# Projecting queries and keys head by head in float32 matmuls of 64 rows

## The chip, the cores and the metric

One core of a Trainium2 chip runs the whole program. The metric is the device time of one execution in microseconds (us); the kernel before takes 731.62 us (median of three runs, 731.14 to 731.96).

## What is computed

Linear attention with a feature map, then two feed-forward stages, on the attention's output laid out as 1152 tokens by 512. All of it is float32, and the last stage's shapes do not matter for this change.

```python
def phi(x):
    proj = np.einsum('bhsd,df->bhsf', x, w_phi)          # head_dim 64 -> 128 features
    proj = proj - np.max(np.abs(proj), axis=-1, keepdims=True)
    return np.concatenate([np.exp(proj), np.exp(-proj)], axis=-1)
q_p, k_p = phi(q), phi(k)                                 # batch 2, heads 8, seq 576
kv = np.einsum('bhsf,bhsd->bhfd', k_p, v)
z = np.sum(k_p, axis=2)
num = np.einsum('bhsf,bhfd->bhsd', q_p, kv)
den = np.einsum('bhsf,bhf->bhs', q_p, z)[..., None] + 1e-06
attn = num / den                                          # -> x, 1152 x 512
y = (x @ w_a * (x @ w_b)) @ w_out                         # d_ff 1536
out = sum over e of p[:, e:e+1] * (max(y @ w1[e], 0) @ w2[e])   # 4 experts
```

## The kernel before

Heads are handled two at a time: a pair p of heads lies one head in partitions 0 to 63, the other in 64 to 127, so that a tile of 128 tokens of one pair is a 128 x 128 block with the head dimension on the partitions. The keys and the queries come in `load_chunk` as chunks of 768 columns; an *item* is 256 columns of a chunk, that is two such tiles j. There are 36 items, 18 of keys (`kind` "k") and then 18 of queries. 576 tokens are four tiles of 128 and a rest of 64, and the rests of two pairs share one tile (marked "m" in `tiles_of_batch`).

The main loop at the end goes over *slots*, and in every slot writes, in this order: the splitting of the raw columns of the item three slots ahead (`split_x`), the projection of this slot's item (`stage_proj`), the key-value sums of the item three slots back (`stage_kv`), for queries the transposes of the item four slots back (`stage_rt`), then what was put off to this slot (`stage_kvz`, `stage_num`, `stage_x`, `stage_xparts`), and in even slots three tasks that prepare later weights (`prep(3)`: ACT, DVE and POOL work on a 512-column half). Every engine takes its instructions in the order in which this loop writes them.

`split_x` makes from each item's float32 columns a high part (ACT, line 84) and a low part (POOL, line 85) in the fast float32r type. `stage_proj` then makes one product of 128 rows against a block-diagonal weight of 256 columns (`wbp`: w_phi for head 0, zeros, and the reverse) out of three float32r matmuls, hi x hi, hi x lo, lo x hi, so that both heads come out of one matmul (lines 166 to 168):

```python
nc.tensor.matmul(out=o, lhsT=hi, rhs=wbp[:, 0], start=True, stop=False)
nc.tensor.matmul(out=o, lhsT=hi, rhs=wbp[:, 1], start=False, stop=False)
nc.tensor.matmul(out=o, lhsT=lo, rhs=wbp[:, 0], start=False, stop=True)
```

DVE takes the largest magnitude (line 171) and subtracts it (line 173); for keys ACT makes two exponentials (lines 179 and 180). `stage_kv` (line 197) sums into PSUM with true float32 matmuls; a full tile uses 128 rows, a shared rest first rows 0 to 63 for both heads of one pair, then rows 64 to 127 for both heads of the next. A float32 matmul is two instructions on PE, a float32r matmul or a transpose is one. When a pair is done, DVE copies its sums out of PSUM (`kvt`, line 207), two slots later PE transposes them (line 218) and DVE (batch 0) or ACT (batch 1) copies them again (`kvz`, lines 221 and 223). Four PSUM buffers ("u") serve the projections, the transposes and the first matmuls of the next stage by turns; two more ("nd") hold the sums. After the loop the two feed-forward stages run as long series of float32r matmuls.

Of the kernel before, what the change touches and what calls it, by code (L numbers as in the profile page):

```python
# [9 lines left out]
F32 = mybir.dt.float32  # L10
F32R = mybir.dt.float32r
U32 = mybir.dt.uint32
AF = mybir.ActivationFunctionType
ALU = mybir.AluOpType
# [33 lines left out]
def tile_linear_attention_then_mlps(ctx, tc, qT, kT, v, w_phi, wab, wout, w12, probs, out):  # L48
# [19 lines left out]
    m_p = None  # L68
    l_p = None

    wb = r_p.tile([128, 2, 128], F32, tag="wb", name="wb")
    wbp = r_p.tile([128, 2, 256], F32R, tag="wbp", name="wbp")

    with tc.manual_schedule():
        nc.scalar.dma_start(out=wb[0:64, 0, :], in_=w_phi)
        nc.scalar.dma_start(out=wb[64:128, 1, :], in_=w_phi)
        nc.vector.memset(wb[0:64, 1, :], 0.0)
        nc.vector.memset(wb[64:128, 0, :], 0.0)

        nc.vector.memset(psm, 0.0)  # L80
        nc.scalar.activation(out=psm, in_=psm, func=AF.Exp)
# [1 line left out]
        def two_parts(hi, lo, src, eng):  # L83
            nc.scalar.activation(out=hi, in_=src, func=AF.Copy)  # L84
            eng.tensor_tensor(out=lo, in0=src, in1=hi.bitcast(F32), op=ALU.subtract)  # L85

        NC = 3 * 256
        xraw = {}
        xpart = {}

        def load_chunk(n):


            if n >= 2 * B * 3:
                return
            t = r_p.tile([128, NC], F32, tag="xraw", name="xraw", bufs=2)
            src = (kT if n < B * 3 else qT)[n % (B * 3)]
            step = 256 if n == 0 else NC
            for c in range(0, NC, step):
                nc.sync.dma_start(out=t[:, c:c + step], in_=src[:, c:c + step])  # L100
            xraw[n] = t

        def split_x(i, eng):
            n, c = i // 3, i % 3 * 256
            if c == 0:
                xpart[n] = [r_p.tile([128, NC], F32R, tag=f"xp{k}", name="xp", bufs=2) for k in range(2)]
            hi, lo = (t[:, c:c + 256] for t in xpart[n])
            if i == 0:
                nc.vector.tensor_copy(hi, xraw[n][:, 0:256])
                nc.vector.tensor_tensor(out=lo, in0=xraw[n][:, 0:256], in1=hi.bitcast(F32), op=ALU.subtract)  # L110
            else:
                two_parts(hi, lo, xraw[n][:, c:c + 256], eng)
            if c == 512:
                load_chunk(n + 2)

        vt = {}

        def alloc_v(b):
            t = k_p.tile([128, 5, NP, 192], F32, tag="v", name="v", bufs=2)
            nc.gpsimd.memset(t[:, :, :, 64:128], 1.0)  # L120
            vt[b] = t

        def load_v(b, st):

            rows = v[b, st * 128:min(S, (st + 1) * 128)]
            n = rows.shape[0]
            for lo in range(0, 128, n):
                o = vt[b][lo:lo + n, st].rearrange("p a c -> p (a c)")
                nc.sync.dma_start(
                    out=o[:, 128:128 + 3 * 192].rearrange("p (a c) -> p a c", c=192)[:, :, 0:128],  # L130
                    in_=rows[:, 1:H - 1, :].rearrange("s (a h) d -> s a (h d)", h=2),
                )
                nc.sync.dma_start(
                    out=o.rearrange("p (a c) -> p a c", c=64)[:, 0:4 * NP - NP:3 * NP - 1, :],
                    in_=rows[:, 0:H:H - 1, :],
                )
# [10 lines left out]
        for kind in "kq":  # L147
            for b in range(B):
                for g in range(9):
                    items.append((kind, b, g, seq[2 * g:2 * g + 2]))  # L150

        st_r = {}
        st_kp = {}
        kv_ps = {}
        kvt_t = {}
        kvz_t = {}
        qp_t = {}

        def stage_proj(i):
            kind, b, g, ts_ = items[i]  # L160
            ps = u_p.tile([128, 2, 2, 128], F32, tag="u", name="pj")
            for j in range(2):
                c = i % 3 * 256 + j * 128
                hi, lo = (t[:, c:c + 128] for t in xpart[i // 3])
                o = ps[:, j].rearrange("p h f -> p (h f)")
                nc.tensor.matmul(out=o, lhsT=hi, rhs=wbp[:, 0], start=True, stop=False)
                nc.tensor.matmul(out=o, lhsT=hi, rhs=wbp[:, 1], start=False, stop=False)
                nc.tensor.matmul(out=o, lhsT=lo, rhs=wbp[:, 0], start=False, stop=True)
            ps4 = ps.rearrange("p t h f -> p (t h) f")
            mx = r_p.tile([128, 4], F32, tag="mx", name="mx", bufs=4)  # L170
            nc.vector.tensor_reduce(out=mx, in_=ps4, op=ALU.max, axis=AX.X, apply_absolute_value=True)
            r = r_p.tile([128, 4, 128], F32, tag="r", name="r", bufs=6)
            nc.vector.tensor_tensor(
                out=r, in0=ps4, in1=mx.unsqueeze(2).to_broadcast([128, 4, 128]), op=ALU.subtract
            )
            st_r[i] = r
            if kind == "k":
                kp = k_p.tile([128, 4, 2, 128], F32, tag="kp", name="kp", bufs=4)
                nc.scalar.activation(out=kp[:, :, 0, :], in_=r, func=AF.Exp)
                nc.scalar.activation(out=kp[:, :, 1, :], in_=r, func=AF.Exp, scale=-1.0)  # L180
                st_kp[i] = kp

        def stage_kv(i):
            kind, b, g, ts_ = items[i]
            kp = st_kp[i]
            done = []
            for j, t in enumerate(ts_):
                if t[0] == "m":
                    parts = [(t[1], 4, 0, 64, False, True), (t[2], 4, 64, 128, True, False)]
                else:  # L190
                    first, last = t[1] == 0, t[1] == 3
                    parts = [(t[0], t[1], 0, 128, first and t[0] % 2 == 0, last and t[0] % 2 == 1)]
                for p, st, lo, hi, first, last in parts:
                    if first:
                        kv_ps[b, p] = nd_p.tile([128, 2, 512], F32, tag="nd", name="kv")
                    for h in range(2):
                        nc.tensor.matmul(
                            out=kv_ps[b, p][:, h, 0:256],
                            lhsT=vt[b][lo:hi, st, p, 64 * h:64 * h + 128],
                            rhs=kp[lo:hi, 2 * j + h].rearrange("p s f -> p (s f)"),  # L200
                            start=first, stop=last,
                        )
                    if last:
                        done.append((b, p))
            for b, p in done:
                t = k_p.tile([128, 2, 256], F32, tag="kvt", name="kvt", bufs=2)
                nc.vector.tensor_copy(t, kv_ps.pop((b, p))[:, :, 0:256])
                kvt_t[b, p] = t
            return done

# [2 lines left out]
        def stage_kvz(b, p):  # L213
            src = kvt_t.pop((b, p))
            ps = u_p.tile([128, 2, 2, 128], F32, tag="u", name="kz")
            for h in range(2):
                for s in range(2):
                    nc.tensor.transpose(out=ps[:, h, s, :], in_=src[:, h, 128 * s:128 * s + 128], identity=ident)
            t = kvz_all[:, b * NP + p].rearrange("p (h s f) -> p h s f", h=2, s=2)
            if b == B - 1:  # L220
                nc.scalar.activation(out=t, in_=ps, func=AF.Copy)
            else:
                nc.vector.tensor_copy(t, ps)
            kvz_t[b, p] = t

        def stage_rt(i):
            kind, b, g, ts_ = items[i]
            r = st_r[i]
            ps = u_p.tile([128, 2, 2, 128], F32, tag="u", name="rt")
            for j in range(2):  # L230
                for h in range(2):
                    nc.tensor.transpose(out=ps[:, h, j, :], in_=r[:, 2 * j + h, :], identity=ident)
            for t in ts_:
                for p in ([t[0]] if t[0] != "m" else t[1:]):
                    if (b, p) not in qp_t:
# [471 lines left out]
        def run(gen, rate, tasks_per):  # L707
# [13 lines left out]


        load_chunk(0)
        load_chunk(1)
        alloc_v(0)
        load_v(0, 0)
        load_v(0, 1)
        make_identity(nc, ident)
        split_x(0, nc.vector)
        nc.vector.tensor_copy(wbp[:, 0], wb.rearrange("p h f -> p (h f)"))  # L730
        nc.vector.tensor_tensor(
            out=wbp[:, 1], in0=wb.rearrange("p h f -> p (h f)"), in1=wbp[:, 0].bitcast(F32), op=ALU.subtract
        )
        for i in range(1, 3):
            split_x(i, nc.vector)
        for st in range(2, 5):
            load_v(0, st)
        alloc_v(1)

        def probabilities():  # L740
# [24 lines left out]
        for slot in range(NI + 9):  # L765
            if slot < NI:
                kind, b, g, ts_ = items[slot]
                if slot + 3 < NI:
                    split_x(slot + 3, nc.gpsimd)
                stage_proj(slot)  # L770
            if slot == NK + 4:
                for fn, a in todo.pop(slot, []):
                    fn(*a)
# [109 lines left out]
```

## Time and profile before

| | |
|---|---|
| median of three runs | 731.62 us |
| the profiled execution | 731.71 us, of which its span is 729.8 us |
| PE busy | 716.4 us (98%) |
| DVE, ACT, POOL busy | 431.0, 325.8, 304.0 us |

The span runs from the first instruction to the last. PE is the matmul engine, PEld its weight loads, which overlap it. [...]

### The profile page before, as it was taken

Reading aid. Unit: us, or ns where it says so; the run is one execution under the profiler, and the core shown is the slowest. Engines: PE = TensorE matmul, PEld = TensorE weight load, DVE = VectorE, ACT = ScalarE, POOL = GpSimd, SP = SyncE. Lnnn points to the kernel's source line nnn. Section 1 sums busy time; section 2 is a strip of 40 time slices with the busy share of each in tenths; the row PEclk is TensorE's granted clock in tenths of the full one; section 3 lists DMA queues with packets and bytes.
Section 4 is the critical chain, followed back from the end, with each engine's and each line's share of the span. In section 5 each row is a group of like instructions: output and inputs, shape, how many; then the busy total and the mean of one; then the engine's idle time right before and its main releaser. Section 6 shows DMA issues by size and latency. Waiting matters only on the chain.

```text
span 729.8 us, 11577 instructions
## 1 busy us (share of the span) xinstructions
PE 716.4 (98%) x4544; PEld 660.2 (90%) x4544; DVE 431.0 (59%) x737; ACT 325.8 (45%) x658; POOL 304.0 (42%) x277
## 2 busy tenths in 40 slices
PE   7999999999999999999899999999999999999998
PEld 6887879999999999999789898988988898989896
DVE  5997987566666664363635454545455545545454
ACT  5787996655444442233644232323233333423221
POOL 3664435554444343312783434434352535343300
PEclk9999999999999999999999999999999999999999
DMA  8643001332323231012031112110111111100003
GB/s 232 190 131 116 1 30 30 116 96 79 115 64 106 64 87 30 11 49 87 3 114 30 43 46 58 30 58 30 58 55 33 31 58 58 30 30 0 1 1 129
DMA packets 37798, 46.18 MB, mean 63 GB/s; under 512 B 5616, under 2 KB 26608, under 8 KB 37744
## 3 DMA queue, kind: packets, MB, share of 16 engines
q1 hardware_dynamic: 37440, 45.25, 20.7%
q8 instruction: 35, 0.57, 0.3%
q10 hardware_dynamic: 304, 0.20, 0.1%
q14 instruction: 19, 0.16, 0.1%
HBM read 43.08 MB, written 2.36 MB: 62 GB/s over the span
## 4 chain that ended last, share of the span: by engine, by line
PE 85%; DVE 8%; ACT 3%; DMA 2%; issue 1%; POOL 0%; DVEq 0%; SPq 0%; POOLq 0%
PE acc L680 9%; PE acc L679 9%; PE acc L678 9%; PE ab L608 6%; PE ab L606 6%; PE ab L607 6%; PE X L531 5%; PE X L532 5%; PE X L533 5%; PE acc L637 3%; PE acc L638 3%; PE acc L636 3%; PE num L275 3%; PE Z L532 2%; PE Z L531 2%; PE Z L533 2%
## 5 line engine op out<-in xcount | busy, mean ns | idle before, releaser
L694 DVE SCALAR_TENSOR_TENSOR oacc<-acc,pr,oacc 128x512 f32<-128x512 f32 (+1 forms) x136 | 101.3, 746 | 117.5 <-PE acc L680 117.5
L85 POOL TENSOR_TENSOR w<-wx,w 128x512 fp32r<-128x512 f32 x68 | 91.5, 1346 | 155.2 <-ACT w L84 155.2
L85 POOL TENSOR_TENSOR wc<-wt,wc 128x512 fp32r<-128x512 f32 (+1 forms) x48 | 70.0, 1490 | 109.6 <-ACT wc L84 109.6
L680 PE MATMUL acc<-w,hhb 128*128 128x512 f32 x288 | 114.0, 396 | 0.9 <-DVE hhb L655 0.9
L606 PE MATMUL ab<-xh,w 128*128 128x288 f32 x384 | 113.5, 296 | 0.0
L608 PE MATMUL ab<-xh,w 128*128 128x288 f32 x384 | 113.1, 295 | 0.0
L679 PE MATMUL acc<-w,hhb 128*128 128x512 f32 x288 | 113.1, 393 | 0.0
L607 PE MATMUL ab<-xl,w 128*128 128x288 f32 x384 | 113.0, 294 | 0.0
L678 PE MATMUL acc<-w,hhb 128*128 128x512 f32 x288 | 112.7, 391 | 0.0
L654 ACT ACTIVATE hhb<-h 128x288 fp32r<-128x288 f32 x64 | 36.2, 565 | 96.2 <-DVE h L539 96.1
L531 PE MATMUL X<-xc,wc 128*128 128x288 f32 x256 | 77.2, 301 | 1.4 <-ACT h L536 1.4
L532 PE MATMUL X<-xc,wc 128*128 128x288 f32 x256 | 75.8, 296 | 0.7 <-DVE xc L85 0.7
L533 PE MATMUL X<-xc,wc 128*128 128x288 f32 x256 | 75.4, 295 | 0.0
L536 ACT ACTIVATE h<-X 128x288 f32<-128x288 f32 x64 | 26.0, 407 | 104.7 <-PE X L533 104.7
L607 PEld LDWEIGHTS ab<-xl,w 128*128 128x128 f32 x384 | 72.0, 188 | 0.1
L606 PEld LDWEIGHTS ab<-xh,w 128*128 128x128 f32 x384 | 72.0, 188 | 0.1
L608 PEld LDWEIGHTS ab<-xh,w 128*128 128x128 f32 x384 | 72.0, 188 | 0.0
L680 PEld LDWEIGHTS acc<-w,hhb 128*128 128x128 f32 x288 | 54.0, 188 | 15.7 <-DVE hhb L655 4.4
L376 POOL TENSOR_TENSOR wx<-wx,rn 128x512 uint32<-128x512 uint32 x36 | 47.0, 1306 | 50.8 <-DVE wx L373 50.8
L655 DVE SCALAR_TENSOR_TENSOR hhb<-h,hhb 128x288 fp32r<-128x288 f32 x64 | 40.5, 633 | 42.2 <-ACT hhb L654 42.2
L679 PEld LDWEIGHTS acc<-w,hhb 128*128 128x128 f32 x288 | 54.0, 188 | 8.4
L678 PEld LDWEIGHTS acc<-w,hhb 128*128 128x128 f32 x288 | 54.1, 188 | 7.7
(104 smaller groups left out, 1655.0 us busy)
## 6 DMA issues: line engine op xcount, KB each, us to landing
raw<-in_wab SPq DMA_DIRECT2D x24, 512.0 KB, 3.8
wt<-in_w SPq DMA_DIRECT2D x64, 128.0 KB, 2.4
wx<-in_w SPq DMA_DIRECT2D x32, 256.0 KB, 3.0
raw<-in_wout SPq DMA_DIRECT2D x12, 512.0 KB, 3.7
xraw<-in_qT SPq DMA_DIRECT2D x6, 384.0 KB, 3.1
out<-oacc SPq DMA_DIRECT2D x8, 256.0 KB, 2.0
xraw<-in_kT SPq DMA_DIRECT2D x5, 384.0 KB, 3.6
v<-in_v SPq DMA_DIRECT2D x8, 192.0 KB, 4.4
```

The source lines that it names most:

```text
L85: eng.tensor_tensor(out=lo, in0=src, in1=hi.bitcast(F32), op=ALU.subtract)
L376: nc.gpsimd.tensor_tensor(out=x, in0=x, in1=r, op=ALU.add)
L531: nc.tensor.matmul(out=ps, lhsT=whi, rhs=xhi, start=first and a == 0, stop=False, skip_group_check=True)
L532: nc.tensor.matmul(out=ps, lhsT=whi, rhs=xlo, start=False, stop=False, skip_group_check=True)
L533: nc.tensor.matmul(out=ps, lhsT=wlo, rhs=xhi, start=False, stop=a == 1, skip_group_check=True)
L606: nc.tensor.matmul(out=t, lhsT=whi, rhs=hi, start=(c == 0), stop=False)
L607: nc.tensor.matmul(out=t, lhsT=whi, rhs=lo, start=False, stop=False)
L608: nc.tensor.matmul(out=t, lhsT=wlo, rhs=hi, start=False, stop=(c == KD - 1))
L678: nc.tensor.matmul(out=acc, lhsT=hi, rhs=w[:, 0, f], start=f == 0, stop=False)
L679: nc.tensor.matmul(out=acc, lhsT=hi, rhs=w[:, 1, f], start=False, stop=False)
L680: nc.tensor.matmul(out=acc, lhsT=lo, rhs=w[:, 0, f], start=False, stop=f == 1)
L694: nc.vector.scalar_tensor_tensor(out=oc, in0=acc[:, c:c + step], scalar=sc, in1=oc, op0=ALU.mult, op1=ALU.add)
```

## The change

The weight is kept in float32, once for partitions 0 to 63 and once for 64 to 127; nothing is split any more, and `xraw` has three buffers and is read by the matmuls. `stage_proj` is called in even slots alone and projects two items: per head h one PSUM buffer for the four tiles of both items, each by one float32 matmul of 64 rows and 128 columns. DVE's and ACT's operations keep their count and shape, but one now covers four tiles of one head. The copies `kvt` and `kvz` all go to ACT. `feat` finds a tile's place in the new layout.

```diff
-            t = r_p.tile([128, NC], F32, tag="xraw", name="xraw", bufs=2)
+            t = r_p.tile([128, NC], F32, tag="xraw", name="xraw", bufs=3)
...
-        def split_x(i, eng):
...
+        def feat(st, i, j, h):
+            return st[i // 2][h][:, 2 * (i % 2) + j]
...
         def stage_proj(i):
-            kind, b, g, ts_ = items[i]
-            ps = u_p.tile([128, 2, 2, 128], F32, tag="u", name="pj")
-            for j in range(2):
-                c = i % 3 * 256 + j * 128
-                hi, lo = (t[:, c:c + 128] for t in xpart[i // 3])
-                o = ps[:, j].rearrange("p h f -> p (h f)")
-                nc.tensor.matmul(out=o, lhsT=hi, rhs=wbp[:, 0], start=True, stop=False)
-                nc.tensor.matmul(out=o, lhsT=hi, rhs=wbp[:, 1], start=False, stop=False)
-                nc.tensor.matmul(out=o, lhsT=lo, rhs=wbp[:, 0], start=False, stop=True)
...
+            for h in range(2):
+                ps = u_p.tile([128, 4, 128], F32, tag="u", name="pj")
+                for n in (i, i + 1):
+                    for j in range(2):
+                        c = n % 3 * 256 + j * 128
+                        nc.tensor.matmul(
+                            out=ps[:, 2 * (n - i) + j], lhsT=xraw[n // 3][64 * h:64 * h + 64, c:c + 128],
+                            rhs=wb[64 * h:64 * h + 64], start=True, stop=True,
+                        )
+                pss.append(ps)
+            for n in (i, i + 1):
+                if n % 3 == 2:
+                    load_chunk(n // 3 + 3)
...
+                r = r_p.tile([128, 4, 128], F32, tag="r", name="r", bufs=8)
...
+                    kp = k_p.tile([128, 4, 2, 128], F32, tag="kp", name="kp", bufs=6)
...
-                nc.vector.tensor_copy(t, kv_ps.pop((b, p))[:, :, 0:256])
+                copy(t, kv_ps.pop((b, p))[:, :, 0:256])
...
-            if b == B - 1:
-                nc.scalar.activation(out=t, in_=ps, func=AF.Copy)
-            else:
-                nc.vector.tensor_copy(t, ps)
+            copy(t, ps)
...
-                if slot + 3 < NI:
-                    split_x(slot + 3, nc.gpsimd)
-                stage_proj(slot)
+                if slot % 2 == 0:
+                    stage_proj(slot)
```

`copy` is an ACT activation. The second chunk is now issued after the first rows of v, the third before the second batch's buffer is set up.

On PE, slots 3 to 5 of the kernel before (pj is a projection's PSUM buffer, kv a sum's, kp the exponentials):

```order
L197 MATMUL kv_208<-kp_149,v_102 128x256 x4
L166 MATMUL pj_215<-wbp_86,xp_134 128x256
L167 MATMUL pj_215<-wbp_86,xp_134 128x256
L168 MATMUL pj_215<-wbp_86,xp_135 128x256
L166 MATMUL pj_215<-wbp_86,xp_134 128x256
L167 MATMUL pj_215<-wbp_86,xp_134 128x256
L168 MATMUL pj_215<-wbp_86,xp_135 128x256
L197 MATMUL kv_208<-kp_165,v_102 128x256 x4
```

and the same place with the change:

```order
L192 MATMUL kv_175<-kp_135,v_97 128x256
L192 MATMUL kv_175<-kp_142,v_97 128x256
L192 MATMUL kv_175<-kp_135,v_97 128x256
L192 MATMUL kv_175<-kp_142,v_97 128x256
L156 MATMUL pj_180<-wb_85,xraw_101 128x128 x4
L156 MATMUL pj_185<-wb_85,xraw_101 128x128 x4
L192 MATMUL kv_175<-kp_135,v_97 128x256
L192 MATMUL kv_175<-kp_142,v_97 128x256
```

Six matmuls in every slot became eight in every second slot, first the four of head 0 (pj_180), then the four of head 1 (pj_185); a sum now reads the exponentials of two buffers.

On ACT, from the first weight tasks on, before:

```order
L84 ACTIVATE xp<-xraw 128x256
L179 ACTIVATE kp<-r 128x4x128
L180 ACTIVATE kp<-r 128x4x128
L84 ACTIVATE xp<-xraw 128x256
L179 ACTIVATE kp<-r 128x4x128
L180 ACTIVATE kp<-r 128x4x128
L84 ACTIVATE w<-wx 128x512
```

and with the change:

```order
L527 ACTIVATE kvt<-kv 128x512
L175 ACTIVATE kp<-r 128x4x128
L176 ACTIVATE kp<-r 128x4x128
L175 ACTIVATE kp<-r 128x4x128
L176 ACTIVATE kp<-r 128x4x128
L81 ACTIVATE w<-wx 128x512
```

The split's two activations are gone and a copy of a pair's sums stands in the queue, here ahead of the four exponentials of two items.

## Rows read from the trace of the kernel before

**Rows 1.** The page: span and busy time of the engines, share, instructions

```profile
span 729.8 us, 11577 instructions
PE 716.4 (98%) x4544; PEld 660.2 (90%) x4544; DVE 431.0 (59%) x737; ACT 325.8 (45%) x658; POOL 304.0 (42%) x277
```

**Rows 2.** Busy time by stretch: PE, PEld, DVE, ACT, POOL, then clock, DMA

```profile
20.00:62.00 42.00, 41.31 (x257) 35.90 (x255) 39.51 (x67) 31.76 (x65) 28.49 (x31) 1.00 0.58 168
62.00:90.00 28.00, 27.47 (x165) 23.56 (x164) 23.08 (x36) 25.36 (x59) 10.90 (x13) 1.00 0.11 32
90.00:130.00 40.00, 38.98 (x240) 34.39 (x239) 31.51 (x49) 31.87 (x66) 17.73 (x12) 1.00 0.12 35
130.00:725.00 595.00, 592.01 (x3807) 551.68 (x3807) 323.50 (x562) 224.66 (x448) 239.72 (x209) 1.00 0.18 53
```

**Rows 3.** Waits of PE, 4 to 130 us: total, times, longest

```profile
PE pj L166 <- DVE wbp L730: 4.6, 1, 4.6
PE pj L166 <- DVE r L173: 0.9, 2, 0.5
```

**Rows 4.** Chain of waits, about 72 us: start, us, work

```profile
71.98 0.12 PE pj L166
72.10 0.12 PE pj L167
...
72.70 0.44 PE rt L232 x4
```

**Rows 5.** Weight loads in time, 15 to 17.3 us: start, us, instructions

```profile
15.09 0.19 PEld L168 LDWEIGHTS pj<-wbp,xp 128*128 128x128 f32 x1
15.41 0.74 PEld L197 LDWEIGHTS kv<-kp,v 64*128 64x128 f32 x8
16.48 0.73 PEld L197 LDWEIGHTS kv<-kp,v 128*128 128x128 f32 x4 [0.33 <-issue]
17.24 0.19 PEld L166 LDWEIGHTS pj<-wbp,xp 128*128 128x128 f32 x1
```

**Rows 6.** The same, 28.9 to 30.7 us, around a sum of full height

```profile
28.92 0.19 PEld L168 LDWEIGHTS pj<-wbp,xp 128*128 128x128 f32 x1
29.04 1.61 PEld L197 LDWEIGHTS kv<-kp,v 128*128 128x128 f32 x8
30.67 0.19 PEld L166 LDWEIGHTS pj<-wbp,xp 128*128 128x128 f32 x1
```

**Rows 7.** Instructions in time, the start: DVE's first, PE, DVE's first largest magnitude

```profile
2.91 0.75 DVE L109 CAST xp<-xraw 128x256 fp32r<-128x256 f32 x1 [1.57 <-DMA xraw<-in_kT]
...
4.56 0.58 PE L166 MATMUL pj<-wbp,xp 128*128 128x256 f32 x1 [4.56 <-DVE wbp L730]
...
6.25 0.41 PE L166 MATMUL pj<-wbp,xp 128*128 128x256 f32 x1
...
6.47 0.41 PE L167 MATMUL pj<-wbp,xp 128*128 128x256 f32 x1
...
6.49 0.69 DVE L171 TENSOR_REDUCE mx<-pj 128x4 f32<-128x512 f32 x1 [0.85 <-PE pj L168]
...
10.09 2.24 PE L197 MATMUL kv<-kp,v 128*128 128x256 f32 x8
```

**Rows 8.** DMA issues: queue, count, KB each, median us to landing

```profile
wb<-in_w_phi ACTq DMA_DIRECT2D x2, 32.0 KB, 2.6
```

**Rows 9.** Groups by shape: count, busy us, mean ns, idle before

```profile
L85 POOL TENSOR_TENSOR xp<-xraw,xp 128x256 fp32r<-128x256 f32 x33 | 24.5, 752 | 19.5 <-ACT xp L84 18.9 <-DMA v<-in_v 0.6
...
L84 ACT ACTIVATE xp<-xraw 128x256 fp32r<-128x256 f32 x35 | 14.2, 411 | 1.5 <-DMA xraw<-in_kT 1.4
...
L179 ACT ACTIVATE kp<-r 128x512 f32<-128x512 f32 x18 | 11.3, 626 | 11.0 <-DVE r L173 10.0 <-PE kv L197 0.5 <-PE pj L168 0.4
...
L207 DVE COPY kvt<-kv 128x512 f32<-128x512 f32 x8 | 5.4, 679 | 0.0
...
L223 DVE COPY kvz<-kz 128x512 f32<-128x512 f32 x4 | 2.7, 680 | 0.0
L221 ACT ACTIVATE kvz<-kz 128x512 f32<-128x512 f32 x4 | 2.3, 587 | 1.9 <-PE kz L218 1.9
```

More of the change, by code (lines that the diff above doesn't have):

```diff
@@ L69, in tile_linear_attention_then_mlps @@
     l_p = None
-    wb = r_p.tile([128, 2, 128], F32, tag="wb", name="wb")
-    wbp = r_p.tile([128, 2, 256], F32R, tag="wbp", name="wbp")
+    wb = r_p.tile([128, 128], F32, tag="wb", name="wb")
     with tc.manual_schedule():
[L75 to L78, printed above, removed]
+        nc.scalar.dma_start(out=wb[0:64], in_=w_phi)
+        nc.scalar.dma_start(out=wb[64:128], in_=w_phi)
         nc.vector.memset(psm, 0.0)
@@ L88, in tile_linear_attention_then_mlps @@
         xraw = {}
-        xpart = {}
         def load_chunk(n):
@@ L101, in load_chunk @@
             xraw[n] = t
-        def split_x(i, eng):
[L104 to L110, printed above, removed]
-            else:
-                two_parts(hi, lo, xraw[n][:, c:c + 256], eng)
-            if c == 512:
-                load_chunk(n + 2)
         vt = {}
@@ L169, in stage_proj @@
[L169 to L181, printed above, removed]
+            kind = items[i][0]
@@ new lines, in stage_proj @@
+            pss = []
+            for h in range(2):
[8 more added lines that the diff above has]
+                pss.append(ps)
@@ new lines, in stage_proj @@
+            for n in (i, i + 1):
+                if n % 3 == 2:
+                    load_chunk(n // 3 + 3)
+            st_r[i // 2], st_kp[i // 2] = [], []
+            for ps in pss:
+                mx = r_p.tile([128, 4], F32, tag="mx", name="mx", bufs=4)
+                nc.vector.tensor_reduce(out=mx, in_=ps, op=ALU.max, axis=AX.X, apply_absolute_value=True)
+                r = r_p.tile([128, 4, 128], F32, tag="r", name="r", bufs=8)
+                nc.vector.tensor_tensor(
+                    out=r, in0=ps, in1=mx.unsqueeze(2).to_broadcast([128, 4, 128]), op=ALU.subtract
+                )
+                st_r[i // 2].append(r)
+                if kind == "k":
+                    kp = k_p.tile([128, 4, 2, 128], F32, tag="kp", name="kp", bufs=6)
+                    nc.scalar.activation(out=kp[:, :, 0, :], in_=r, func=AF.Exp)
+                    nc.scalar.activation(out=kp[:, :, 1, :], in_=r, func=AF.Exp, scale=-1.0)
+                    st_kp[i // 2].append(kp)
@@ L183, in stage_kv @@
         def stage_kv(i):
             kind, b, g, ts_ = items[i]
-            kp = st_kp[i]
             done = []
@@ L199, in stage_kv @@
                             lhsT=vt[b][lo:hi, st, p, 64 * h:64 * h + 128],
-                            rhs=kp[lo:hi, 2 * j + h].rearrange("p s f -> p (s f)"),
+                            rhs=feat(st_kp, i, j, h)[lo:hi].rearrange("p s f -> p (s f)"),
                             start=first, stop=last,
@@ L219, in stage_kvz @@
             t = kvz_all[:, b * NP + p].rearrange("p (h s f) -> p h s f", h=2, s=2)
-            if b == B - 1:
-                nc.scalar.activation(out=t, in_=ps, func=AF.Copy)
-            else:
-                nc.vector.tensor_copy(t, ps)
+            copy(t, ps)
             kvz_t[b, p] = t
@@ L227, in stage_rt @@
             kind, b, g, ts_ = items[i]
-            r = st_r[i]
             ps = u_p.tile([128, 2, 2, 128], F32, tag="u", name="rt")
@@ L231, in stage_rt @@
                 for h in range(2):
-                    nc.tensor.transpose(out=ps[:, h, j, :], in_=r[:, 2 * j + h, :], identity=ident)
+                    nc.tensor.transpose(out=ps[:, h, j, :], in_=feat(st_r, i, j, h), identity=ident)
             for t in ts_:
@@ L723, in tile_linear_attention_then_mlps @@
         load_chunk(0)
-        load_chunk(1)
         alloc_v(0)
         load_v(0, 0)
+        load_chunk(1)
         load_v(0, 1)
         make_identity(nc, ident)
[L729 to L735, printed above, removed]
         for st in range(2, 5):
             load_v(0, st)
+        load_chunk(2)
         alloc_v(1)
```

## The prediction

> **What bounds the kernel now.** I read the page first: PE is busy 716.4 of 729.8 us [rows 1]. A busy share alone does not say that PE is the bound in the stage that the change touches, so I went on to the busy time by stretch [rows 2]: the keys' part (20 to 62 us) has PE at 41.31 of 42.00, the queries' part 27.47 of 28.00, then 38.98 of 40.00, and from 130 us on 592.01 of 595.00. DVE is close behind in the keys' part (39.51) and ACT in the queries' (25.36). The third view, PE's waits, tells whether these neighbours hold PE up [rows 3]: 4.6 us once, at the very start, and 0.9 us in two waits of a projection for DVE. So PE has a full queue from 4.56 us to the end. What the change does to the time is then, nearly, what it does to the sum of PE's own work, plus what it does to the start, plus any wait that it makes. Work taken from DVE, ACT and POOL is worth at most the PE waits that it ends.
>
> What a matmul costs on PE is the distance between starts. A projection's float32r matmul of 256 columns costs 0.12 us, a transpose of 128 columns 0.44 / 4 = 0.11 [rows 4]. [...]
>
> **The change, part by part.** *Removed from PE*: per two items, 12 float32r matmuls of 0.12 us, 1.44 us.
>
> *Added to PE*: per two items 8 float32 matmuls of 64 rows, that is 16 instructions of 128 columns. The trace has no projection of this kind, but it has the 64-row sums of the shared rests. There, from the last projection's load at 15.09 to the next projection's at 17.24, 8 instructions of 64 rows and 4 of 128 rows pass in 2.15 us [rows 5]. At another place 8 of 128 rows alone pass in 30.67 - 28.92 = 1.75 us, and by the loads in between (29.04 to 30.67) each is 1.63 / 8 = 0.20 us [rows 6]. Had the 64-row instructions run one after the other, 12 would have passed in about 1.75 + 4 x 0.20 = 2.55. If they run two at a time (rows 0 to 63 beside rows 64 to 127), they count as 4, the sum is the 1.75 us of 8, and 0.40 us is left: the price of changing between 128 and 64 rows and back. The 8 loads of 64 rows also pass in 0.74 us [rows 5], where 8 of 128 rows take 1.61 [rows 6]. I take two at a time.
>
> In the new projection each of these instructions streams 128 columns where the sums stream 256. The nearest row for a float32 stream of 128 columns with its own weight load is the transpose, 0.11; the 0.12 of the projection before is the upper end, and a pair that costs no less than one sum's instruction, 0.20, is out of reach, since a transpose with as large a load costs 0.11. So two items cost 8 pairs x 0.11 + 0.40 = 1.28 us; with 0.12 it is 1.36. Against 1.44 that is 0.16 or 0.08 less. A visit that costs less than 0.40, because the next sum begins with a shared rest and stays in 64 rows (one place) or because the last load is hidden, gives up to 0.23 less. I take 0.15, and 18 pairs of items give 2.7 us less PE work, with 1.4 and 4.1 as ends.
>
> [...]
>
> *The start.* Before, PE waits until 4.56 for DVE to cast the input (from 2.91) and the weight [rows 7]. Now it needs only the loads: the weight's two loads take 2.6 us each from issue [rows 8], the first input is there at 2.91, so the first matmul can start about 3.3, some 1.2 us earlier. But the first sum (10.09 before) now needs both heads of two items: the first four largest magnitudes and subtractions on DVE at about 0.69 each, starting near 5.5 instead of 6.49, then exponentials of 0.63 [rows 7, 9]: about 9.5. [...] Between a gain of 1.2 and a loss of 1.5 I take a gain of 0.5.
>
> *Removed from the other engines*: 35 splits of 0.41 on ACT (14.2 us), 33 of 0.75 on POOL (24.5), and on DVE 8 copies kvt and 4 kvz, 5.4 + 2.7 = 8.1 us. *Added*: those 12 copies on ACT at 0.587 each, 7.0 us [rows 9]. PE's work covers all of it; what it may be worth is DVE's part in PE's waits, 0.9 us [rows 3]. The copies on ACT have the four exponentials of a pair ahead of them in the queue, in even slots, and the projection now comes in lumps of two, so I count 0.5 gained, with 1.5 gained (the PE waits after 62 us too) and nothing as ends. The loads of the inputs move by a few places on SP's queue; PE's waits show none for an input load after the start, with two buffers, and there are three now.
>
> *Sum*, against the profiled execution's 731.71 us: -2.7 - 0.5 - 0.5 = -3.7, **728.0 us**. That execution lies 0.09 us above the median of 731.62, which I neglect. From the ends the same case reaches from 731.71 - 4.1 - 1.2 - 1.5 = 724.9 to 731.71 - 1.4 + 1.5 = 731.8.
>
> **The rivals.** *A: one at a time (slower).* The program writes four matmuls of head 0 and then four of head 1. If PE takes them strictly in that order, only the last instruction of head 0 runs beside the first of head 1, and two items cost 15 x 0.11 + 0.40 = 2.05 us, 0.61 more than 1.44; 18 times that is 11.0, and with the same start and waits 731.7 + 11.0 - 1.0 = 741.7 us. For it: the distance between the two heads' instructions is twice that of the sums, where two matmuls of one half stand ahead of two of the other. Against it: the sums are also written one half after the other and still pass in 2.15 instead of 2.55 [rows 5, 6]. It decides from the second pair on that comes apart: each costs 0.11 more, and the gain of 0.15 in a visit is gone. [...]
>
> *B: ACT holds up the sums (same or slower).* The copy kvt frees a PSUM buffer of the sums. On ACT it stands behind up to four exponentials, 4 x 0.63 = 2.5 us, which wait for DVE. A buffer is needed again two slots later, about 5 us at two slots' PE work. If DVE runs over 2 us behind, three or four such places of batch 1 wait 1.5 us each: 728.0 + 6 = 734. For it: DVE's 39.51 of 42.00 [rows 2]. Against it: DVE loses 8.1 us just there.
>
> *C: the pairing is partial or the visit is dearer.* With two of eight pairs lost in each visit (0.22 x 18 = 4.0) it comes to 732: no change.
>
> **How the numbers follow.** The forecast's case (two at a time, no new wait) has 0.70, A 0.14, B 0.08, C 0.08. A measurement of this kernel can tell about 0.2%, 1.5 us, from no change: faster means below 730.1. The forecast's case ends above that only at its upper end, C and B give same and slower: faster 0.70, same 0.10, slower 0.20. For the range I take the forecast's case with its lower end widened by a little to 723.5, and reach to B and C, 736; A is left out with 0.14.
>
> **What would show it.** Right: PE's loads of 64 rows at line 156 stand two by two, and a visit to the projection takes about 1.3 us from the load before to the load after; PE's first matmul starts near 3.3 us; DVE's busy time falls by at least 8 us, POOL's by 24; the queries' first transposes come about 2 us earlier. Wrong: a visit of 2 us or more (A), PE waits on ACT's kvt (B), or matmul distances of 0.2 beyond 13 us (the clock).

## The result and the profile after

The changed kernel takes 735.95 us (median of four runs, 735.51 to 736.97) where the kernel before takes 731.38 (730.84 to 731.96): a ratio of 1.0064, with a 95% interval of 1.0047 to 1.0082. It is 4.6 us slower; 728.0 was forecast, and the result lies at the top of the given range, on the other side of no change. The profiled execution of the changed kernel, from which the rows below are, took 736.97 us and is the longest of the four.

The page of the changed kernel, first part; it answers to [rows 1]:

```profile
span 735.2 us, 11625 instructions
...
PE 722.0 (98%) x4616; PEld 661.3 (90%) x4616; DVE 421.9 (57%) x717; ACT 321.2 (44%) x635; POOL 279.6 (38%) x244
```

DVE fell by 9.1 us and POOL by 24.4, as expected, and PE, the bound, rose by 5.6. The same stretches as in [rows 2] (length, then busy time of PE, PEld, DVE, ACT, POOL, then clock and DMA), and ahead of them the first one:

```profile
4.50:20.00 15.50, 13.07 (x73) 10.32 (x71) 8.18 (x13) 7.65 (x14) 0.00 (x0) 1.00 0.86 254
20.00:62.00 42.00, 42.00 (x277) 35.22 (x278) 31.02 (x54) 31.63 (x58) 16.36 (x13) 1.00 0.54 153
62.00:90.00 28.00, 27.98 (x182) 23.31 (x183) 21.12 (x34) 18.79 (x42) 1.43 (x1) 1.00 0.14 43
```

In the keys' part DVE is now idle for 11 of 42 us, and PE has not a hundredth to spare. The clock column reads 1.00 in the first row too, although the instructions of the first sum stand 0.427 us apart there, up to 13.5 us, and 0.216 later: at the start the distances tell the rate, not the column. Below, half rate is the first distance and full rate the second; that the clock makes the difference is read from e4, where the sum at 9.64 us goes at 0.41 and the column shows 0.50 (under the start's runs). PE's waits up to 140 us:

```profile
PE pj L156 <- DMA wb<-in_w_phi: 3.1, 1, 3.1
PE pj L156 <- DMA xraw<-in_kT: 2.4, 1, 2.4
PE rt L223 <- ACT qp L241: 0.8, 1, 0.8
...
```

Against [rows 3]: the start begins earlier (3.1 for 4.6 us), both waits for DVE are gone, and a wait for an input chunk has come, right behind the start. None of these rows explains 4.6 us. PE's own order of time does. One visit to the projection in the keys' part (start, duration, instructions; the shown durations of neighbours overlap, as the first row ends at 31.71 and the second starts at 31.64, so that costs are taken from start to start):

```profile
31.05 0.66 PE L213 MATMUL kz<-ident,kvt 128*128 128x128 f32 x4
31.64 1.71 PE L156 MATMUL pj<-wb,xraw 64*128 64x128 f32 x16
33.28 0.70 PE L192 MATMUL kv<-kp,v 128*128 128x256 f32 x2
```

From its first instruction to the next matmul a visit takes 33.28 - 31.64 = 1.64 us, and 15 of the 16 visits after the first two show this number or more; the other joins a shared rest. Two at a time, 8 pairs of 0.11 should have taken 0.9 to 1.1. In the trace's single records the first instruction of head 0 starts at 31.64 and the first of head 1 at 32.19; from there on instructions stand side by side. Up to that moment six loads and five matmuls have begun, eleven of head 0's sixteen (a window that ends at 32.189 us):

```profile
31.64 0.74 PEld L156 LDWEIGHTS pj<-wb,xraw 64*128 64x128 f32 x6 [0.17 <-issue]
31.64 0.82 PE L156 MATMUL pj<-wb,xraw 64*128 64x128 f32 x5
```

So head 0 runs alone for five of its eight matmul instructions, the two overlap in the middle, and head 1 then ends alone.

Where the 5.4 us between the two profiled spans (735.2 and 729.8) come from, by three points of the program that both traces show:

| reached by PE | before | after | later by |
|---|---|---|---|
| last instruction of the sums ahead of slot 6's projection | 17.24 | 19.52 | 2.3 |
| first transposes of the queries | 61.61 | 66.34 | 4.7 |
| end of the span | 729.8 | 735.2 | 5.4 |

The start adds 2.3 us, the middle stretch, nine visits, 2.4, and the rest, six visits among it, 0.7. A second trace of the changed kernel (e0, below) has these points at 18.30, 65.11 and 734.0: the middle adds 2.4 and the rest 0.7 once more, but the start only 1.1. So the two later parts repeat, and the start differs from one execution to the next.

### The profile page after: what moved, and what is told of

Its sections match the earlier page's. It is cut to its first block, busy times and chain, and to the rows that moved or that the text cites. A ratio compares the mean times of both kernels' runs of the same rounds, so it can differ in the third digit from the quotient of the medians.

```text
span 735.2 us, 11625 instructions
## 1 busy us (share of the span) xinstructions
PE 722.0 (98%) x4616; PEld 661.3 (90%) x4616; DVE 421.9 (57%) x717; ACT 321.2 (44%) x635; POOL 279.6 (38%) x244
## 4 chain that ended last, share of the span: by engine, by line
PE 92%; DVE 3%; ACT 3%; issue 1%; DMA 1%; SPq 0%; POOL 0%; DVEq 0%; ACTq 0%; POOLq 0%
PE acc L671 9%; PE acc L670 9%; PE acc L669 9%; PE ab L599 6%; PE ab L597 6%; PE ab L598 6%; PE kv L192 5%; PE X L522 5%; PE X L523 5%; PE X L524 5%; PE pj L156 4%; PE acc L628 3%; PE acc L629 3%; PE acc L627 3%; PE num L266 3%; PE Z L522 2%
```

## Experiments

Each run is set against the kernel before on the same chip: 732.64 us beside e1, e2, e3 and e5, 732.79 beside e0, e4, e8 and e9, 731.93 beside e6 and e10. Across these three chips, ratios are what can be compared.

### e1: the heads by turns

```diff
-            for h in range(2):
-                ps = u_p.tile([128, 4, 128], F32, tag="u", name="pj")
-                for n in (i, i + 1):
-                    for j in range(2):
+            pss = [u_p.tile([128, 4, 128], F32, tag="u", name="pj") for h in range(2)]
+            for n in (i, i + 1):
+                for j in range(2):
+                    for h in range(2):
...
```

> The changed kernel with its eight matmuls of a visit written head 0, head 1, head 0, head 1, tile by tile. Theory P (reach: PE starts an instruction of the other 64 rows beside the current ones only when it stands at most some eight loads and matmuls behind, and the four matmuls of one head are sixteen): all eight run two at a time, a visit of 16 matmuls falls from 1.64 us to about 1.1 (8 x 0.11 and the first one's 0.2), 18 visits give 9 to 10 us, so 726 us. Rival W (the second head waits for its PSUM buffer, which the split order hides): the first two instructions of head 0 run, then all wait for that buffer, the visit stays at about 1.6 us, 735 to 737 us. Rival D (64-row instructions of a projection do not pair at all beyond what the changed trace shows, because their streams of 128 columns are bound by the loads): 735 us.

Measured: 729.49 us, ratio 0.996 (0.9946 to 0.9974). One order of eight matmuls turns a slower kernel into a faster one. The visit that corresponds to the one above:

```profile
28.20 0.66 PE L211 MATMUL kz<-ident,kvt 128*128 128x128 f32 x4
28.78 1.16 PE L155 MATMUL pj<-wb,xraw 64*128 64x128 f32 x16
29.87 0.70 PE L190 MATMUL kv<-kp,v 128*128 128x256 f32 x2
```

It takes 29.87 - 28.78 = 1.09 us, as theory P said. Head 1's first matmul, which would have to wait for the second PSUM buffer, is now the second of the visit and not the fifth, and in the visit at 18.07 us it starts 7 ns behind head 0's (single records); a wait for that buffer (W) would have held it there. W and D fall. The time is 3.5 us above P's 726: 1.3 of it is the chip, on which the kernel before is that much slower too, and two visits among the queries still take 1.48 and 1.64 us, at 61 and 64 us.

### e2 and e10: in twos and in threes

```diff
-                for j in range(2):
-                    for h in range(2):
+                for h in range(2):
+                    for j in range(2):
```

This is e2, against e1. In e10 the order is three tiles of head 0, three of head 1, then one of each (`for group in ((0, 1, 2), (3,))`, then head, then tile).

> The changed kernel with the matmuls of a visit in groups of two, as the sums have them: two of head 0, two of head 1, and again. Theory P: the other head stands eight loads and matmuls behind, as in the shared rests of the sums, which pair from the first; the visit takes about 1.1 us as with full alternation and the time is within 1 us of it, about 726 us. If the reach is shorter than eight, the visit lies between, near 1.3 us, and the time near 730. Rival W: 1.6 us and 735 to 737 us.

> The changed kernel with a visit's matmuls written three of head 0, three of head 1, then one of each. Theory P with the reach that the traces show (head 1 starts when five or six loads and matmuls that stand ahead of it are left): head 1 starts about 0.3 us after head 0, a visit takes about 1.35 us, between 1.19 with groups of two and 1.64 with groups of four; some 731 to 733 us. Rival W (a wait for the second PSUM buffer): 1.6 us as with groups of four, or 1.1 as with alternation, but nothing between.

Measured: e2 730.51 us, ratio 0.9971 (0.9958 to 0.9984); e10, one run, 733.30, a little over the forecast of 731 to 733. A visit and the matmul after it in e2, then in e10:

```profile
19.06 1.26 PE L155 MATMUL pj<-wb,xraw 64*128 64x128 f32 x16
20.25 0.48 PE L190 MATMUL kv<-kp,v 128*128 128x256 f32 x1
```

```profile
18.93 1.49 PE L155 MATMUL pj<-wb,xraw 64*128 64x128 f32 x16
20.34 0.48 PE L190 MATMUL kv<-kp,v 128*128 128x256 f32 x1
```

A visit takes 1.09, 1.19, 1.41 and 1.64 us for groups of one, two, three and four. That is graded, as a reach makes it, and not either-or, as a wait would. The reach of eight that P took for e1 is too long: by it groups of two should have taken about 1.1, and they took 1.19. By the single records, head 1 starts in groups of three when seven of the twelve loads and matmuls ahead of it have begun, in groups of four when eleven of sixteen have: five are left both times. In the shared rests of the sums before the change, in twos, the other half's load starts 13 ns after the first one, with six of eight left (a window from 15.41 to 15.43 us):

```profile
15.41 0.20 PEld L197 LDWEIGHTS kv<-kp,v 64*128 64x128 f32 x2
15.41 0.49 PE L197 MATMUL kv<-kp,v 64*128 64x256 f32 x2
```

So in these traces an instruction for the other 64 rows starts when no more than five or six older ones wait ahead of it. For such instructions PE does not keep the order in which the loop writes them, as was said of every engine at the outset: head 1 of the changed kernel starts at 32.19 us, with five instructions of head 0 still ahead. What sets the reach inside the engine no run shows.

### e8: no split, but 128 rows

```diff
-                nc.tensor.matmul(out=o, lhsT=hi, rhs=wbp[:, 0], start=True, stop=False)
-                nc.tensor.matmul(out=o, lhsT=hi, rhs=wbp[:, 1], start=False, stop=False)
-                nc.tensor.matmul(out=o, lhsT=lo, rhs=wbp[:, 0], start=False, stop=True)
+                nc.tensor.matmul(
+                    out=ps[:, j].rearrange("p h f -> p (h f)"), lhsT=xraw[i // 3][:, c:c + 128],
+                    rhs=wb.rearrange("p h f -> p (h f)"), start=True, stop=True,
+                )
...
```

The base is the kernel before; the splitting is taken out, `xraw` has three buffers and is loaded earlier, and the copies are ACT's.

> No split, float32, but 128 rows: the kernel before with its block-diagonal weight left in float32, one float32 matmul of 256 columns per tile on the raw input, each item in its own slot, copies on ACT. A tile costs two instructions of 0.216 us, two items 1.73 us on PE, with no change between 64 and 128 rows. Theory M (a visit to the projection in the changed kernel costs 1.64 us and about 0.2 more for going in and out, 1.84): this is 18 x 0.11 = 2 us faster than the changed kernel and 18 x 0.3 = 5.5 us of PE work more than before, less 2 to 4 us at the start and in waits that end, 733 to 735 us. Theory C (work on 64 rows does not raise the clock, 128 rows do): the higher clock comes before 10.8 us, since PE starts at about 3.1. Rival to M (the cost of the change is the loss at the start alone): equal to the kernel before or faster, under 732 us.

Measured: 734.24 us, ratio 1.0025 (1.0014 to 1.0036), 2.0 us less than the changed kernel beside it (e0, 736.25). In order of time (PE alone):

```profile
18.07 1.03 PE L149 MATMUL pj<-wb,xraw 128*128 128x256 f32 x4
18.93 1.89 PE L183 MATMUL kv<-kp,v 128*128 128x256 f32 x8
20.66 1.03 PE L149 MATMUL pj<-wb,xraw 128*128 128x256 f32 x4
```

An item costs 18.93 - 18.07 = 0.86 us and two items 1.72, and nothing is lost around them. Theory M is borne out: with its heads in fours, the 64-row projection is no better than a full-height float32 one with half of its products wasted on zeros. The rival, that the start alone is to blame, forecast no more than the kernel before and falls, since this kernel is slower by 1.8 us (1.0 to 2.6). In its trace the three points of the table above lie at 17.86, 63.32 and 732.2: the start adds 0.6 us, the middle 1.1 and the rest 0.7. PE starts at 5.06, not at 3.1 as expected.

### e0, e3, e4, e9: the start

e3 issues the second input chunk ahead of the rows of v, e4 does that and alternates the heads, e9 is e4 with five matmuls on a constant tile ahead of the first projection:

```diff
         load_chunk(0)
-        alloc_v(0)
-        load_v(0, 0)
         load_chunk(1)
+        alloc_v(0)
+        load_v(0, 0)
         load_v(0, 1)
```

```diff
+        warm = r_p.tile([128, 512], mybir.dt.bfloat16, tag="warm", name="warm")
+        nc.vector.memset(warm, 1.0)
+        wps = u_p.tile([128, 512], F32, tag="u", name="wps")
+        for _ in range(5):
+            nc.tensor.matmul(out=wps, lhsT=warm[:, 0:128], rhs=warm, start=True, stop=True)
```

> The changed kernel with the second input chunk issued right behind the first, ahead of the rows of v, as before the change. Theory S (start: PE's 2.4 us wait for this chunk at 6.3 to 8.8 us makes the first sum late, and the idle PE gets the higher clock only at 13.3 us instead of about 10.3): the first sum starts near 9.6 instead of 10.8 us, half rate ends earlier, and the time falls by 1 to 2.5 us, to 733.5 to 735. Rival (the rows of v are then late by as much as the chunk was, the first sum waits for them instead): no difference, 735.5 to 736.5 us.

> The changed kernel itself, unaltered, on the same chip as the three beside it, so that they can be set against it. All theories: 1.006 of the kernel before. In its trace the higher clock is granted at some 13 to 15 us, as in the changed kernel and its variants so far (12.0 to 14.9), where the kernel before has 10.8.

> Alternating heads and the second input chunk issued right behind the first, both at once. Theory P and S together: the two gains add, 0.996 from alternation and 1.4 us (0.9980) from the load order, 0.994 of the kernel before, about 728 us if that is at 732.5. Rival: with alternation PE is no longer behind at the start, so the earlier chunk gives nothing more, 0.996.

> The kernel with alternating heads and the earlier chunk, and in addition five matmuls of 128 rows and 512 columns on a constant tile ahead of the first projection, whose result nobody reads. Theory C: the higher clock is granted earlier, at about 7 to 11 us, so that the first sums run at 0.216 instead of 0.427 us an instruction; 1 to 2 us less than with alternation and the earlier chunk alone. Rival (the time of the rise is chance): no difference beyond 0.5 us.

| run | what | us | ratio (95%) | first sum: start, and how long its 8 instructions pass |
|---|---|---|---|---|
| e0 | the changed kernel | 736.25 | 1.005 (1.0033 to 1.0067) | 10.18, 2.80 |
| e3 | earlier chunk | 735.31 | 1.0045 (1.0027 to 1.0063) | 8.79, 3.78 |
| e4 | alternation, earlier chunk | 728.91 | 0.9951 (0.9933 to 0.9969) | 8.37, with waits inside |
| e9 | e4 and constant matmuls | 728.97 | 0.9941 (0.9923 to 0.9958) | 8.21, with waits inside |

PE in order of time at the start, of the changed kernel and then of e3:

```profile
3.07 3.26 PE L156 MATMUL pj<-wb,xraw 64*128 64x128 f32 x20 [3.07 <-DMA wb<-in_w_phi]
8.77 2.09 PE L156 MATMUL pj<-wb,xraw 64*128 64x128 f32 x12 [2.43 <-DMA xraw<-in_kT]
10.78 3.42 PE L192 MATMUL kv<-kp,v 128*128 128x256 f32 x8
```

```profile
3.15 5.72 PE L156 MATMUL pj<-wb,xraw 64*128 64x128 f32 x32 [3.15 <-DMA wb<-in_w_phi]
8.79 3.78 PE L192 MATMUL kv<-kp,v 128*128 128x256 f32 x8
```

The first half of theory S holds in the trace: the wait of 2.4 us goes and the first sum starts 1.4 us earlier than in e0 and 2.0 earlier than in the first trace of the changed kernel. But its eight instructions then take 3.78 us, all at half rate (the next matmul starts at 12.51, 3.72 us later, 0.465 each), where they took 2.24 before the change [rows 7], partly at full rate. In time, e3 and e0 cannot be told apart, nor e4 and e1: their intervals overlap. The order of the loads is worth at most a microsecond or so, and what it gives is taken back at half rate: the last instruction of the sums ahead of slot 6 starts at 18.28 in e3 and at 18.30 in e0.

When the clock rises, read from these distances, is what the traces leave open. The changed kernel alone has it at two times: in its first trace the instructions of the first sum stand 0.427 us apart up to 13.5 us, in e0 only up to 11.6, and 0.216 from 11.96 on, where 13 to 15 was expected for the rise. In e8, whose projections use 128 rows, the first sum already runs at full rate at 10.76 us (12.48 - 10.76 = 1.72 us to the next matmul, 0.215 each):

```profile
5.06 5.87 PE L149 MATMUL pj<-wb,xraw 128*128 128x256 f32 x16 [5.06 <-DMA wb<-in_w_phi]
10.76 1.89 PE L183 MATMUL kv<-kp,v 128*128 128x256 f32 x8
```

and in e9, after the constant matmuls, the projections themselves are at full rate from 5.0 us on; here PE in e9 and then in e4:

```profile
1.45 2.31 PE L81 MATMUL wps<-warm 128*128 128x512 bf16 x5 [1.45 <-DVE psm L83]
3.70 2.97 PE L161 MATMUL pj<-wb,xraw 64*128 64x128 f32 x32
8.21 0.67 PE L196 MATMUL kv<-kp,v 128*128 128x256 f32 x2 [1.55 <-ACT kp L180]
```

```profile
3.10 4.20 PE L155 MATMUL pj<-wb,xraw 64*128 64x128 f32 x32 [3.10 <-DMA wb<-in_w_phi]
8.37 0.67 PE L190 MATMUL kv<-kp,v 128*128 128x256 f32 x2 [1.07 <-ACT kp L174]
9.64 2.52 PE L190 MATMUL kv<-kp,v 128*128 128x256 f32 x6 [0.61 <-ACT kp L174]
```

Both agree with theory C, that the clock rises later behind work on 64 rows than behind work on 128. But e4 speaks against it: its projections pass at 0.21 us a pair until 6.5 us and at 0.11 from 6.7 on, so there the clock rose on 64-row work alone. It then fell again after a stretch in which PE was busy for 1.62 of 3.30 us (e4 by stretch; the granted clock stands ahead of the last two), and the sum at 9.64 us, whose next matmul starts at 12.10, goes at 2.46 / 6 = 0.41:

```profile
6.70:10.00 3.30, 1.62 (x13) 1.03 (x12) 3.23 (x6) 2.53 (x5) 0.00 (x0) 1.00 0.97 241
10.20:13.50 3.30, 3.30 (x17) 2.42 (x17) 0.82 (x2) 1.86 (x4) 0.00 (x0) 0.50 0.81 248
```

That is one trace of each, so C is left open. In its trace e9 is 2.6 us ahead of e4 at the first transposes of the queries (57.81 against 60.41), and 0.7 at the end (spans of 727.0 and 727.7); between them lies a stretch of half rate at 353 us, shown in the last section. Over six and seven executions the times of e9 and e4 do not differ, and so the constant matmuls are not shown to pay.

### e5 and e6: the copies

```diff
-                copy(t, kv_ps.pop((b, p))[:, :, 0:256])
+                nc.vector.tensor_copy(t, kv_ps.pop((b, p))[:, :, 0:256])
```

e5 undoes this, and `kvz` of batch 0 likewise, in the changed kernel; e6 makes the same two edits the other way round in the kernel before.

> The changed kernel with the copies kvt on DVE and kvz of batch 0 on DVE, as before the change. Theory: the copies on ACT cost nothing and give little, since PE shows no wait on either engine between 13 and 98 us; the time stays within 1 us of the changed kernel, 735 to 737 us. Rival (moving them is what ended PE's waits of 55 to 62 us before the change): 1 to 2 us more, 737 to 738 us.

> The kernel before with its copies kvt and kvz on ACT and nothing else changed. Theory (DVE's copies are what makes PE wait at 55 to 62 us, and nothing else hangs on them): PE's waits for line 173 there, 0.9 us, go, and the time is 0.5 to 1.5 us less, 0.998 to 0.9995 of the kernel before. Rival B of the prediction (behind the exponentials on ACT the copies come late and the sums wait): slower by 1 us or more.

Measured: e5 737.03 us, ratio 1.0063 (1.0045 to 1.0081), the same as the changed kernel's 1.0064, though the time itself touches the rival's 737; e6 731.26 us, ratio 0.999 (0.9979 to 1.0001), which may be a small gain or none. PE's waits in e6, from 4 to 130 us:

```profile
PE pj L166 <- DVE wbp L727: 4.4, 1, 4.4
PE kv L197 <- ACT kvt L533: 0.7, 1, 0.7
PE num L272 <- ACT x L284: 0.5, 1, 0.5
...
```

The two waits for DVE [rows 3] are gone, and one of 0.7 us for the copy on ACT has come, rival B's mechanism in small. The copies are worth nothing that can be measured either way.

## Why the prediction was wrong, step by step

**The step that failed** is "I take two at a time", and with it the 1.28 us for a visit. The price was taken from the shared rests of the sums, where the two halves stand two matmuls apart; the projection writes them four apart. I had named that difference under rival A and still gave A 0.14. The truth lies between: a visit takes 1.64 us; going in, its first instruction starts 0.20 us behind the last transpose instead of 0.11, and going out, the second full-height instruction starts 0.32 behind the first instead of 0.22 (33.28 + 0.70 less its own 0.38). That makes 1.64 + 0.09 + 0.10 = 1.83, where I had 1.28 for the forecast and 2.05 for A. Against 1.44 it is 0.39 more, not 0.15 less: 18 visits, 7.0 us instead of -2.7. That is an error of 9.7 us in one term, and the whole miss is 8. In the trace the first two visits lie in the start, at half rate; the other sixteen make 5.6 us (0.4 + 3.8 + 1.4, below), the rest of the start 1.9, and stops that ended take off 2.1, together the 5.4 between the spans. That 735.95 is still inside the range is largely luck: its upper end was taken from B and C at their own prices, not from dearer visits and a late start.

That the rest of the term was sound is shown by e1: 1.09 + 0.09 + 0.10 = 1.28 us, the very figure of the forecast, once the heads stand by turns. The whole sum was -3.7 us; e1 measured 0.4% less than the kernel before, 2.9 us (1.9 to 4.0).

**The price of changing between 128 and 64 rows** (0.40 taken, from [rows 5, 6]) was right: in e1 it is 0.19 at the edges and, inside, 1.09 instead of 8 x 0.11 = 0.88, which makes 0.40. e8 does not test it: that its 1.72 us beat 1.83 comes of the pairs that were lost, since with all of them the visit takes 1.28. The good end of this term, 0.23 less a visit, was worked out from no row.

**The start** was forecast 0.5 us better, with a loss of 1.5 as the bad end. The sums ahead of slot 6 come 2.3 us later, of which one visit's excess is 0.4; in e0 1.1. What I had missed is the chunk: "PE's waits show none for an input load after the start" was read from a kernel that asked for the second chunk before v and needed it in the fourth slot; projecting in pairs needs it in the third, and the change had put it behind two loads of v. But that wait is not shown to be the price: e3 has none and is no earlier than e0 at slot 6. Half rate lasted longer than before: 3.42 us for eight instructions where [rows 7] has 2.24. The loss of 1.5 was my estimate and no run shows it; what they showed in its place is 2.3 and 1.1 us at slot 6.

**The other engines' part** was forecast to give 0.5 us, 1.5 at most. In the middle stretch nine visits (items 6 to 23) cost 9 x 1.83 = 16.5 us, some 0.4 less because one joins a shared rest; before, items 6 to 22 cost 17 x 0.72 = 12.2 there. So 3.8 should have been added, and 2.4 came. After it six visits, which end ahead of transposes (0.09 + 1.64 + 0.06 = 1.79), cost 10.7 for the 9.4 of the 13 items left; 1.4 should have been added, and 0.7 came. So about 2 us of small stops of before went away. By e6 the copies are at most a fraction of it: with them alone the middle is 0.4 us shorter and the rest 0.1. e8, without the splits too, agrees: an item 0.14 dearer should have added 2.4 and 1.8 there, and 1.1 and 0.7 came. That the splits did most of it is likely but was not tried alone.

**The rivals**: A's condition was right and its price too high, 2.05 us a visit where 1.83 came, since overlap is not lost altogether; B was seen only in e6, 0.7 us; C, partial pairing, named exactly what happened, but with two of eight pairs lost, at 732 us, where (1.64 - 1.09) / 0.11 = five of eight were.

## What to carry to other kernels

Here two matmuls on 64 rows each ran beside each other only where they stood close in the program (they started with at most five or six older loads and matmuls left ahead): write the halves by turns, one of each, 1.09 us a visit here for 1.64. (In e1 each half has its own PSUM buffer; whether it needs one was not tried.) A price read from one place of a trace holds for the distance, the order and the queue state it was read at; when a change copies the mechanism but not the distance, look at how the price depends on it first. Where PE is full (42.00 of 42.00 us in the keys' part here), a change that frees other engines is paid for by PE's own order of instructions, and the row to read is the time from the first matmul of a visit to the first one after it. The changed kernel with its heads by turns beats both kernels: 0.996 (0.9946 to 0.9974), and with the earlier chunk 0.9951 (0.9933 to 0.9969).

## What the runs showed of the hardware that was not expected

The reach: five or six older loads and matmuls stood ahead of an instruction for the other 64 rows when it started; with groups of one, two, three and four a visit of sixteen instructions took 1.09, 1.19, 1.41 and 1.64 us. It shows at the start of the changed kernel as well: at 8.77 us, behind the wait for the chunk, head 0 has two tiles left, eight instructions, and head 1 starts 14 ns after the first of them, with six left, as in the sums.

The clock fell in the middle of a run: in e9's profiled execution the granted share was 0.90 and 0.67 in the two stretches after a gap of PE at 350 us, where e4 and the kernel before, with a gap at about the same place, kept 1.00 (stretch, its length, busy times, granted clock ahead of the last two):

```profile
350.00:354.00 4.00, 2.01 (x11) 1.78 (x12) 2.11 (x3) 2.79 (x6) 1.20 (x1) 0.90 0.01 2
354.00:358.00 4.00, 4.00 (x23) 3.99 (x22) 0.60 (x2) 2.38 (x6) 3.92 (x3) 0.67 0.01 4
```

PE is busy for 2 of 4 us in the first of these stretches, and the fall shows in the next: from 353.2 to 356.6 us the granted clock is 0.50. What brought it about these rows do not tell, for the kernel before is busy for 2.03 of 4.00 us from 354 to 358 and keeps 1.00. It cost e9 most of what it had gained at the start: its lead on e4 is 2.6 us still at 302 us and 0.7 at 369.
